# A Fourier-filter prologue and the last units of a two-matrix block: GpSimd and ScalarE steps moved earlier, sums reordered, filler products added

## The chip, the core and the metric

The kernel runs on one core of a Trainium2 chip. The core has five engines with a queue of instructions each: TensorE (PE in the profile; its weight loads are PEld) multiplies matrices into PSUM; VectorE (DVE) and ScalarE (ACT) work on PSUM and SBUF; GpSimd (POOL) works on SBUF; SyncE (SP) issues transfers. ScalarE and GpSimd issue transfers too. The metric is the device time of one execution in microseconds, as the median of several runs.

## What is computed

```python
def _attn_ref(x, filt_r, filt_i):            # x: (8, 3008, 256); filters: (1505, 256)
    X = np.fft.rfft(x, axis=1)
    F = (filt_r + 1j * filt_i)[None, :, :]
    return np.fft.irfft(X * F, n=x.shape[1], axis=1).astype(np.float32)

def _moe_ref(x, w_in, w_out):                # x: (24064, 256); w_in: (256, 2048); w_out: (2048, 256)
    h = x @ w_in
    g = h - np.tanh(h)
    return (g @ w_out).astype(np.float32)
```

The second function takes the first one's output, its eight batches laid end to end. The weights w_in and w_out arrive as 64-bit floats.

## The kernel before

**The transform.** A sequence of 3008 is 47 rows of 64. For each batch the transform runs in steps of small products: along the 64 ("first"), along the 47 ("forth"), the pointwise filter ("filtered"), and the two ways back ("back", "last"). The 32 frequencies along the 64 are cut into seven groups of five (`SLOTS`; the last has two, and its two halves of the columns are stacked, which gives 96 rows instead of 120). Group 0 to group 6 are handled one after the other.

**The prologue** does batch 0 with all data in SBUF, and ends where the main part begins. Per group g it issues, in this order: the loads of the filter rows of group g+2 (`filters_of`); the transposes of group g+2 (`across`, L1050, copied by L1054); the products of group g+1 (`there0`, L411 into the banks pa and pb; pa is copied by ScalarE, L414); the sum and difference of group g on VectorE (`next(there[g][0])`, L416 and L417, which read pb and the copy); three conversion steps (`convert(3)`); the filter of group g (`filtered`: L428, L433, L434, L435 on VectorE, then L437, by GpSimd for groups 1 to 4 and by VectorE for groups 0, 5 and 6; group 6 goes on with the sums L439 and L440); and the way back of the group before (`way_back`: L1087 and L1089 into the bank pe, copied by L1092, stored by L1093 to an array in memory). `back` (L459, L462, L464) does the same for group 6. Group 5's and group 6's ways back come last; then `rest` loads what all groups stored (L1077), four `first1` products of batch 1 run (L1175), 14 products that nobody reads (`warmer`, L1038) and the main part's first products (L576).

**The conversion** of the weights from 64 to 32 bits (`converted`) is a chain of steps per job of 512 words a row: a load (L174), one ScalarE step (L180), then VectorE steps L182, L185, L188, L191, L193 and a sum L200. `early` steps through the first five jobs, one step per call: five calls ahead of the group loop, behind group 0's transposes and in front of group 0's `there0`, three in each of groups 0 to 4, three at the start of group 5, and what is left behind the loop. `late` does the other jobs in the main part; there the ScalarE step of job k+1 is taken in the middle of job k.

**The filter rows turned.** Two rows of the last group come in the other order from memory, the imaginary one negated (`turned_rows`): GpSimd issues a load `neg` and one write (L531) ahead of the loop. At the end of group 2 VectorE negates (L540), GpSimd stores the result to `less` in memory (L541) and at once issues the write that reads `less` (L531). Two weight loads (`ahead`, L174) follow on GpSimd's queue. `filters_of(6)` reads what was written (L1067).

**The main part** is 192 units. Unit U multiplies by w_in (`up`, L617, seven products in place of eight), applies h - tanh h by an approximation (`shrink`: L729, L732, L735 on ScalarE, L739 on VectorE for each half of the columns, then four sums L597 to L600), and multiplies by w_out (`down`, L787, seven products). The stages of one unit overlap those of the next two: U's `up` is interleaved with U-1's `shrink` and U-2's `down` through the calls `d`, `e`, `s`, `t`. `steps_at` says how many steps of `shrink` run at each of eight places of `up`. The order of every engine's queue is that of the program. `down` collects four units in PSUM; the fourth ends with sums (L801 to L821), and the very last is turned and stored by `store_last` (L885, L886, L888).

What the change touches, in the names of the lines above: `weights` (L249), `turned_rows` (L540 to L542), `steps_at` (L626), `shrink` (ahead of L761), `down` (L798 to L821), `store_last` (L882 to L890), and the group loop (L1215 to L1236).

Of the kernel before, what the change touches and what calls it, by code (L numbers as in the profile page):

```python
# [18 lines left out]
NQ, NR = 64, 47  # L19
# [97 lines left out]
def kernel(  # L117
# [123 lines left out]
    def weights(tiles, jobs, queue, began, ahead, after=()):  # L241

        began += [begun(tiles, job, queue) for job in jobs[len(began):ahead]]
        yield
        for k in range(len(jobs)):
            pending[0] = len(jobs) - k
            for n, _ in enumerate(began[k]):
                yield
                if after and n == 2 and k + 1 < len(jobs):  # L249
                    next(began[k + 1])  # L250
            if k + ahead < len(jobs):
                began.append(begun(tiles, jobs[k + ahead], queue))
            pending[0] = len(jobs) - k - 1
            for u in dict(after).get(k, ()):
                yield from sums(u)
# [272 lines left out]
    def turned_rows(t):  # L528

        def turned_to(v, src, top):  # L530
            G.dma_start(dram(filt_d, (turned * 8 + 5 + 2 * v) * DM,  # L531
                             [[DM // 2, 2], [8 * DM, NH], [1, DM // 2]]),
                        dram(src, top * DM, [[DM // 2, 2], [(top > NH and -NQ or -1) * DM, NH],
                                             [1, DM // 2]]))

        G.dma_start(t, dram(filt_i.tensor, (SEQ // 2 - NQ * (NH - 1)) * DM,
                            [[NQ * DM, NH], [1, DM]]))
        turned_to(0, filt_r.tensor, SEQ // 2)
        yield
        V.tensor_scalar(out=t, in0=t, scalar1=-1.0, scalar2=None, op0=ALU.mult)  # L540
        G.dma_start(dram(less_d, 0, [[DM, NH], [1, DM]]), t)  # L541
        turned_to(1, less_d, NH - 1)  # L542
        yield

# [59 lines left out]
    def up(U, d, e, s, t):  # L604

        i, u = divmod(U, 4)
        b, tu, w = uts[i]
        rhs = [b[0][0], b[1][0], b[1][1], tu[:, 3, 0:w], tu[:, 0, 0:w], tu[:, 1, 0:w],
               tu[:, 2, 0:w]]
        banks = {k: ps.tile([128, 2, 256], F32, tag=k, bufs=1, name=k) for k in "xyz"}  # L610
        X, Y, Z = (banks[k][:, :, 0:w] for k in "xyz")
        h = dn.tile([128, 4, 2, 256], F32, tag="h", bufs=3, name="h")
        hs[U] = (h, w)

        def mm(bank, q, first):
            for k in range(2):
                nc.tensor.matmul(bank[:, k], wu[:, q - 1, (2 * u + k) * 128:(2 * u + k + 1) * 128],  # L617
                                 rhs[q - 1], start=(first and k == 0), stop=True,
                                 skip_group_check=True)

        def copied(tag):
            t = dn.tile([128, 2, 256], F32, tag=tag, bufs=1, name=tag)[:, :, 0:w]
            ACT.copy(t, X)  # L623
            return t

        steps_at = ([1, 1, 1, 1, 0, 1, 1, 0] if U > 1 else [0, 0, 1, 0, 2, 0, 2, 1])  # L626

        close = groups[i][0] == 0

        def shrinks(at):  # L630
            for _ in range(steps_at[at]):
                s()

        mm(X, 1, True)
        mm(Y, 2, True)
        s1 = copied("s1")
        t(0)
        d()
        shrinks(0)
# [12 lines left out]
        shrinks(3)  # L652
        e()
        t(2)
        mm(X, 7, False)
        u3 = copied("u3")
        V.tensor_add(h[:, 3, :, 0:w], Z, u3)  # L657
        shrinks(4)
        d()
        shrinks(5)  # L660
        e()
        if close:
            t(3)
        mm(X, 4, False)
        V.tensor_copy(h[:, 2, :, 0:w], X)  # L665
        if not close:
            t(3)
        shrinks(6)
        d()
        e()  # L670
        t(4)
        mm(Z, 3, False)
        V.tensor_add(h[:, 1, :, 0:w], Z, u2)  # L673
        shrinks(7)
# [42 lines left out]
    def shrink(U):  # L717
# [39 lines left out]
            return  # L757
        t = dn.tile([128, 4, 2, 256], F32, tag="t", bufs=2, name="t")
        blocks = [[h[:, 2 * a + k, :, 0:w] for k in range(2)] for a in range(2)]

        combine(blocks, [t[:, k, :, 0:w] for k in range(4)],  # L761
                V if pending or U + 2 >= 4 * len(groups) else G)
# [5 lines left out]
    def down(U):  # L768
# [24 lines left out]
        if done:  # L793
# [1 line left out]
                          for k in ("p1", "p5", "pu2"))  # L795
            o = dn.tile([128, 2, CH * 128], F32, tag="o", bufs=1, name="o")
            x12 = o[:, 0, w:2 * w]
        mm(1, 2)  # L798
        yield
        if done:  # L800
            ACT.copy(p1, product(1))  # L801
            V.tensor_add(o[:, 0, 0:w], product(2), p1)
        yield
        mm(3, 5)
        yield
        if done:
            ACT.copy(p5, product(5))
            V.tensor_add(x12, product(3), p5)
# [3 lines left out]
        if done:  # L812
            V.tensor_add(u2, product(6), p1)
            V.tensor_add(p1, product(7), u2)
            G.tensor_add(x12, u2, x12)  # L815
        yield
        mm(4)
        yield
        if done:
            V.tensor_add(o[:, 1, 0:w], product(4), p1)  # L820
            G.tensor_add(o[:, 1, w:2 * w], p1, p5)  # L821
            accs.pop(i)
            if i + 1 < len(groups):
                stores.append((i, o))
# [53 lines left out]
    def store_last(i, o):  # L878

        b, c = groups[i]  # L880
        ot = dn.tile([128, CH, DM], F32, tag="ot", bufs=1, name="ot")
        for h, copy in ((0, ACT.copy), (1, V.tensor_copy)):  # L882
            pt = psl([128, CH, 128], "xy"[h])
            for j in range(CH):
                nc.tensor.transpose(pt[:, j], o[:, h, j * 128:(j + 1) * 128], one)  # L885
            copy(ot[:, :, h * 128:(h + 1) * 128], pt)  # L886
        for (r, step, m, j, half), queue in zip(runs(c), (nc.sync, ACT)):
            queue.dma_start(dram(out.tensor, (b * SEQ + r) * DM,  # L888
                                 [[NR * DM, 64], [step * DM, m], [1, DM]]),
                            ot[64 * half:64 * half + 64, j:j + m])  # L890

    def store_some(n):
        for dst, src in outs[:n]:
# [95 lines left out]
    with tc.tile_pool(name="tr", bufs=2) as tr, tc.manual_schedule():  # L989
# [16 lines left out]
        with tc.tile_pool(name="pro", bufs=1) as pro, \  # L1006
# [201 lines left out]
            for g in range(last_g + 1):  # L1208
# [5 lines left out]
                    ones_1 = first1(load_x(big([128, 8, DM], F32, "x1"), 1, 0, 8))  # L1214
                if g == last_g - 1:  # L1215
                    under(fts[last_g])
                    convert(3)
                    way_back()
                if g < last_g:
                    there[g + 1] = there0(g + 1)  # L1220
                next(there[g][0])
                if g < last_g - 1:
                    convert(3)
                xy = there.pop(g)[1]
# [4 lines left out]
                if g in summed:  # L1229
                    next(chain)  # L1230
                ended.append((back, (0, g, xy, z0, (ACT, nc.sync))) if g in summed else (back0, (g, nn)))
                if g not in (0, last_g - 1):
                    way_back()
                if g == 2:
                    next(turning)
                    ahead = [begun(tiles1, job, queue=G) for job in jobs[5:7]]  # L1236
            rest(0, SG * (last_g - 1), [nc.sync])
            way_back()
            rest(SG * (last_g - 1), NA - SG * (last_g - 1), [nc.sync])
# [207 lines left out]
```

## Time and profile before

| | |
|---|---|
| median of 3 runs | 2564.09 us (2563.33 to 2565.52) |
| the profiled execution | 2566.24 us |
| its span, first to last instruction | 2564.4 us |
| mean granted TensorE clock | 0.996 |
| GpSimd busy | 58% |
| DMA, mean over the span | 83 GB/s |
| prologue (start to the first L576) | 87.6 us |
| the last store's issue | 2557.1 us |

A row of the timeline has start and duration in us, engine, line, operation, what is written and read, the shape, and in brackets the idle time of the engine ahead of it with what ended it. A row of waits has the total, the number and the longest. SPq, ACTq and POOLq are the queues that issue transfers. A 32-bit product of 256 columns shows as two records.

### The profile page before, as it was taken

The page shows a single profiled execution, that of the slowest core. Times are in us where ns is not written, and L with a number is a line of the kernel's source. Part 1 is how long each engine was busy: PE and PEld are TensorE (multiplying, and loading weights), DVE is VectorE, ACT ScalarE, POOL GpSimd, SP SyncE. Part 2 cuts the span into 40 slices and gives each one's busy share as a digit, 9 for nine tenths or more (in the row PEclk, how much of TensorE's full clock was granted, in tenths as well). Part 3 has the DMA queues.
Part 4 walks back from the last instruction along what each step waited for, and adds up shares of the span by engine and source line. Part 5 has one row for each costly group of instructions (what it writes and reads, how often), then busy time and mean ns, then how long its engine had stood idle before and what let it go on. Part 6 is the DMA issues. An engine that isn't in the chain of part 4 may idle for free.

```text
span 2564.4 us, 44624 instructions
## 1 busy us (share of the span) xinstructions
PE 2540.9 (99%) x17076; PEld 2177.8 (85%) x17076; DVE 1878.4 (73%) x2265; ACT 1666.3 (65%) x2497; POOL 1481.4 (58%) x1124
## 2 busy tenths in 40 slices
PE   8999999999999999999999999999999999999998
PEld 7678888888898888988888888898889888898887
DVE  6788776887678876788668886688866877555555
ACT  4566666666666666666666666676666666666665
POOL 4256665666466655666656665566645666555552
PEclk9999999999999999999999999999999999999999
DMA  8873214422343323342233322443123322110110
GB/s 221 260 198 103 65 35 109 119 67 48 76 118 93 80 54 94 82 108 67 72 94 90 92 67 61 101 105 97 36 64 88 93 66 52 26 32 18 26 21 19
DMA packets 333660, 212.43 MB, mean 83 GB/s; under 512 B 231737, under 2 KB 304855, under 8 KB 329789
## 3 DMA queue, kind: packets, MB, share of 16 engines
q1 hardware_dynamic: 318511, 184.59, 29.5%
q0 software_dynamic: 11424, 17.03, 2.4%
q10 hardware_dynamic: 3502, 7.87, 0.9%
q8 instruction: 136, 2.23, 0.4%
q14 instruction: 87, 0.71, 0.1%
HBM read 128.75 MB, written 83.39 MB: 83 GB/s over the span
## 4 chain that ended last, share of the span: by engine, by line
PE 94%; DMA 2%; DVE 1%; ACT 1%; issue 1%; POOL 0%; ACTq 0%; POOLq 0%; DVEq 0%
PE o L787 43%; PE x L617 25%; PE z L617 12%; PE y L617 6%; PE pm L401 3%; PE pu L576 2%; DMA ct<-a 1%; PE pm L340 1%; DMA raw<-in_moe_w_in_dram 0%; DMA fh<-f 0%; DMA mats_sb<-mats 0%; PE pe L1089 0%; PE o L842 0%; PE pf L297 0%; PE warm L1038 0%
## 5 line engine op out<-in xcount | busy, mean ns | idle before, releaser
L787 PE MATMUL o<-t,wd 128*128 128x256 f32 (+1 forms) x3008 | 763.6, 377 | 0.0
L597 POOL TENSOR_TENSOR t<-h 128x512 f32<-128x512 f32 (+1 forms) x186 | 305.7, 1643 | 712.4 <-DVE h L739 703.9
L739 DVE TENSOR_TENSOR h<-h,y 128x1024 f32<-128x1024 f32 (+1 forms) x384 | 579.8, 1510 | 160.8 <-ACT y L735 157.3
L787 PEld LDWEIGHTS o<-t,wd 128*128 128x128 f32 x3008 | 569.3, 190 | 85.3 <-POOL o L815 15.1
L617 PE MATMUL x<-tu,wu 128*128 128x256 f32 (+1 forms) x2256 | 576.2, 378 | 0.2 <-ACT u L623 0.2
L787 PE MATMUL o<-h,wd 128*128 128x256 f32 (+1 forms) x2256 | 573.6, 377 | 1.8 <-DVE h L739 1.8
L787 PEld LDWEIGHTS o<-h,wd 128*128 128x128 f32 x2256 | 426.0, 190 | 72.8 <-issue 18.4
L623 ACT COPY s<-x 128x512 f32<-128x512 f32 (+1 forms) x188 | 108.6, 578 | 564.6 <-PE x L617 564.6
L617 PEld LDWEIGHTS x<-tu,wu 128*128 128x128 f32 x2256 | 423.6, 190 | 57.2 <-issue 3.7
L732 ACT ACTIVATE y<-y 128x1024 f32<-128x1024 f32 (+1 forms) x384 | 399.4, 1040 | 12.1
L735 ACT ACTIVATE y<-y 128x1024 f32<-128x1024 f32 (+1 forms) x384 | 399.8, 1041 | 4.6
L729 ACT ACTIVATE y<-h 128x1024 f32<-128x1024 f32 (+1 forms) x384 | 400.5, 1043 | 3.6 <-DVE h L665 1.7
L598 POOL TENSOR_TENSOR t<-h,t 128x512 f32<-128x512 f32 (+1 forms) x186 | 313.9, 1688 | 14.6
L600 POOL TENSOR_TENSOR t<-h,t 128x512 f32<-128x512 f32 (+1 forms) x186 | 303.7, 1633 | 0.0
L599 POOL TENSOR_TENSOR t<-h 128x512 f32<-128x512 f32 (+1 forms) x186 | 289.7, 1557 | 0.0
L623 ACT COPY u<-x 128x512 f32<-128x512 f32 (+1 forms) x376 | 213.3, 567 | 57.0 <-PE x L617 53.7
L665 DVE COPY h<-x 128x512 f32<-128x512 f32 (+1 forms) x188 | 127.8, 680 | 127.2 <-PE x L617 127.1
L617 PE MATMUL z<-tu,wu 128*128 128x256 f32 (+1 forms) x752 | 190.2, 376 | 0.4 <-DVE h L673 0.4
L617 PE MATMUL z<-ut,wu 128*128 128x256 f32 (+1 forms) x752 | 190.2, 376 | 0.4 <-DVE h L657 0.4
L617 PE MATMUL y<-ut,wu 128*128 128x256 f32 (+1 forms) x752 | 190.2, 376 | 0.0
L617 PE MATMUL x<-ut,wu 128*128 128x256 f32 (+1 forms) x752 | 190.2, 376 | 0.0
L657 DVE TENSOR_TENSOR h<-z,u 128x512 f32<-128x512 f32 (+1 forms) x188 | 127.2, 677 | 72.1 <-ACT u L623 71.1
(198 smaller groups left out, 2815.7 us busy)
## 6 DMA issues: line engine op xcount, KB each, us to landing
ft<-filt SPq DMA_DIRECT2D x28, 1024.0 KB
ct<-nn SPq DMA_DIRECT2D x56, 512.0 KB
e<-ct SPq DMA_DIRECT2D x47, 512.0 KB
a<-ct SPq DMA_DIRECT2D x112, 192.0 KB
out_dram<-ot SPq DMA_DIRECT2D x1248, 16.0 KB
x_sb<-in_x_dram SPq DMA_DIRECT2D x110, 128.0 KB
ct<-a SPq DMA_DIRECT2D x60, 128.0 KB
ct<-x_sb SPq DMA_DIRECT2D x60, 128.0 KB
```

What stands on the lines that cost most here:

```text
L597: by.tensor_sub(t[0], b[0][1], b[0][0])
L598: by.tensor_sub(t[1], b[1][1], t[0])
L599: by.tensor_sub(t[2], b[1][1], b[0][1])
L600: by.tensor_sub(t[3], b[1][0], t[1])
L617: nc.tensor.matmul(bank[:, k], wu[:, q - 1, (2 * u + k) * 128:(2 * u + k + 1) * 128], rhs[q - 1], start=(first and k == 0), stop=True, ski ...
L623: ACT.copy(t, X)
L665: V.tensor_copy(h[:, 2, :, 0:w], X)
L729: ACT.activation(y[k], ht[k], AF.Arctan, scale=TURN)
L732: ACT.activation(y[k], y[k], AF.Tanh, scale=BEND)
L735: ACT.activation(y[k], y[k], AF.Square, scale=SCALE, accum_out=y_sums[:, 2 * U + k // 2:2 * U + k // 2 + 1])
L739: V.tensor_mul(ht[k], ht[k], y[k])
L787: nc.tensor.matmul(product(q), wd[:, q - 1, (2 * u + k) * 128: (2 * u + k + 1) * 128], rhs[q - 1][:, k], start=(u == 0 and k == 0 and q == ...
```

## The change

- `weights`: the ScalarE step of the next job is taken in the middle of the current one for the early jobs too, not only for the late ones.
- `turned_rows`: the negation runs on GpSimd, and the store of `less` and the write that reads it are in two steps. The first is called at the end of group 1, the second at the end of group 2. The two `ahead` loads are issued at group 3, in front of its `way_back`.
- Group 5: its L416 and L417 are issued first, then four filler products, then the way back of group 4; its three conversion steps move to its end, behind three more filler products.
- `steps_at` has a seventh step; it has work only in the last unit's `up`, where the four sums of the unit before come behind `up`'s last sum (L673).
- `down` of the last unit takes its products in the order 2, 3, 1, 5, 6, 7, 4; its sums follow, one of them moves from GpSimd to VectorE, and one GpSimd sum is issued earlier.
- `store_last` works by halves of the rows instead of halves of the columns: each is turned, copied and stored by two transfers, the second half of the rows first.

```diff
@@ weights
-                if after and n == 2 and k + 1 < len(jobs):
+                if n == 2 and k + 1 < len(jobs):
                     next(began[k + 1])
@@ turned_rows
         yield
-        V.tensor_scalar(out=t, in0=t, scalar1=-1.0, scalar2=None, op0=ALU.mult)
+        G.tensor_scalar(out=t, in0=t, scalar1=-1.0, scalar2=None, op0=ALU.mult)
         G.dma_start(dram(less_d, 0, [[DM, NH], [1, DM]]), t)
+        yield
         turned_to(1, less_d, NH - 1)
@@ up
-        steps_at = ([1, 1, 1, 1, 0, 1, 1, 0] if U > 1 else [0, 0, 1, 0, 2, 0, 2, 1])
+        steps_at = ([1, 1, 1, 1, 0, 1, 1, 1] if U > 1 else [0, 0, 1, 0, 2, 0, 2, 1])
@@ shrink
+        if U + 2 == 4 * len(groups):
+            yield
         combine(blocks, ...)
@@ down
-        mm(1, 2)
+        last_unit = U + 1 == 4 * len(groups)
+        mm(*((2, 3) if last_unit else (1, 2)))
         yield
-        if done:
+        if done and not last_unit:
             ACT.copy(p1, product(1))
             V.tensor_add(o[:, 0, 0:w], product(2), p1)
         yield
-        mm(3, 5)
+        mm(*((1, 5) if last_unit else (3, 5)))
         yield
+        if last_unit:
+            ACT.copy(p1, product(1))
+            V.tensor_add(o[:, 0, 0:w], product(2), p1)
...
-            G.tensor_add(x12, u2, x12)
+            (V if last_unit else G).tensor_add(x12, u2, x12)
+            if last_unit:
+                G.tensor_add(o[:, 1, w:2 * w], p1, p5)
...
-            G.tensor_add(o[:, 1, w:2 * w], p1, p5)
+            if not last_unit:
+                G.tensor_add(o[:, 1, w:2 * w], p1, p5)
@@ store_last
-        for h, copy in ((0, ACT.copy), (1, V.tensor_copy)):
-            pt = psl([128, CH, 128], "xy"[h])
-            for j in range(CH):
-                nc.tensor.transpose(pt[:, j], o[:, h, j * 128:(j + 1) * 128], one)
-            copy(ot[:, :, h * 128:(h + 1) * 128], pt)
-        for (r, step, m, j, half), queue in zip(runs(c), (nc.sync, ACT)):
...
+        for lo, tag, copy in ((2, "x", ACT.copy), (0, "y", V.tensor_copy)):
+            pt = psl([128, 2, DM], tag)
+            for h in range(2):
+                for j in range(2):
+                    nc.tensor.transpose(pt[:, j, h * 128:(h + 1) * 128],
+                                        o[:, h, (lo + j) * 128:(lo + j + 1) * 128], one)
+            copy(ot[:, lo:lo + 2], pt)
+            for (r, step, m, j, half), queue in zip(runs(c), (nc.sync, ACT)):
...
@@ the group loop
                 if g == last_g - 1:
                     under(fts[last_g])
-                    convert(3)
+                    next(there[g][0])
+                    warmer(4)
                     way_back()
                 if g < last_g:
                     there[g + 1] = there0(g + 1)
-                next(there[g][0])
+                if g != last_g - 1:
+                    next(there[g][0])
...
+                if g == 3:
+                    ahead = [begun(tiles1, job, queue=G) for job in jobs[5:7]]
                 if g not in (0, last_g - 1):
                     way_back()
-                if g == 2:
+                if g in (1, 2):
                     next(turning)
-                    ahead = [begun(tiles1, job, queue=G) for job in jobs[5:7]]
+                if g == last_g - 1:
+                    warmer(3)
+                    convert(3)
```

More of the change, by code (lines that the diff above doesn't have):

```diff
@@ L881, in store_last @@
         ot = dn.tile([128, CH, DM], F32, tag="ot", bufs=1, name="ot")
-        for h, copy in ((0, ACT.copy), (1, V.tensor_copy)):
-            pt = psl([128, CH, 128], "xy"[h])
-            for j in range(CH):
-                nc.tensor.transpose(pt[:, j], o[:, h, j * 128:(j + 1) * 128], one)
-            copy(ot[:, :, h * 128:(h + 1) * 128], pt)
-        for (r, step, m, j, half), queue in zip(runs(c), (nc.sync, ACT)):
-            queue.dma_start(dram(out.tensor, (b * SEQ + r) * DM,
-                                 [[NR * DM, 64], [step * DM, m], [1, DM]]),
-                            ot[64 * half:64 * half + 64, j:j + m])
+        for lo, tag, copy in ((2, "x", ACT.copy), (0, "y", V.tensor_copy)):
[6 more added lines that the diff above has]
+            for (r, step, m, j, half), queue in zip(runs(c), (nc.sync, ACT)):
+                queue.dma_start(dram(out.tensor, (b * SEQ + r + step * lo) * DM,
+                                     [[NR * DM, 64], [step * DM, 2], [1, DM]]),
+                                ot[64 * half:64 * half + 64, j + lo:j + lo + 2])
     def store_some(n):
```

## The prediction

> **What bounds the kernel now.** I read the page first, then the waits of TensorE, then the granted clock by microsecond, then the timeline of the prologue (0 to 88 us) and of the last 25 us.
>
> ```profile
> PE 2540.9 (99%) x17076; PEld 2177.8 (85%) x17076; DVE 1878.4 (73%) x2265; ACT 1666.3 (65%) x2497; POOL 1481.4 (58%) x1124
> ...
> PE 94%; DMA 2%; DVE 1%; ACT 1%; issue 1%; POOL 0%; ACTq 0%; POOLq 0%; DVEq 0%
> ...
> PE pe L1089 <- POOL nn L437: 5.4, 2, 4.3
> PE pe L1087 <- DVE nn L434: 1.8, 1, 1.8
> ```
>
> TensorE is busy for 99% of the span and 94% of the chain. A change that takes no product away can win only TensorE's idle time and its slow time. The idle time that lies late in the prologue is in the rows above (one pause of 4.3 us, one of 1.8 us); one more pause of 1.56 us, shown below, lies at the very end. The slow time is in the windows (columns: busy time and count of PE, PEld, DVE, ACT, POOL, then granted clock, DMA share, GB/s):
>
> ```profile
> 56.00:57.00 1.00, 0.00 (x0) 0.00 (x0) 1.00 (x1) 0.00 (x0) 1.00 (x1) 0.74 0.88 191
> ...
> 63.00:64.00 1.00, 1.00 (x6) 0.81 (x5) 0.00 (x0) 0.42 (x1) 0.32 (x1) 0.84 0.17 42
> ...
> 70.00:71.00 1.00, 0.43 (x3) 0.17 (x2) 0.96 (x3) 0.00 (x0) 0.09 (x1) 0.57 0.90 135
> ...
> 76.00:77.00 1.00, 1.00 (x4) 0.66 (x3) 0.96 (x2) 0.00 (x0) 0.00 (x0) 0.52 0.61 213
> ```
>
> After each prologue pause the clock halves (at about 56.5 and 70.1) and comes back at about 63.3 and 77.0, so two stretches of about 6.8 us run at 0.50. Where the first pause comes from:
>
> ```profile
> 53.73 0.68 POOL L531 DMA_DIRECT2D filt<-less  x1 [5.17 <-DMA less<-neg]
> 53.83 0.68 DVE L188 SCALAR_TENSOR_TENSOR top<-raw,top 128x512 int32<-128x512 int32 x1
> ...
> 55.00 2.72 DVE L193 SCALAR_TENSOR_TENSOR low<-raw,low 128x512 f32<-128x512 uint32 x1
> ...
> 55.88 1.29 POOL L437 TENSOR_TENSOR nn<-nn,xy 120x512 f32<-120x512 f32 x1
> ...
> 57.22 0.47 PEld L1089 LDWEIGHTS pe<-nn,mats_sb 120*120 120x120 f32 x2 [4.67 <-POOL nn L437]
> ...
> 57.65 1.21 DVE L428 TENSOR_TENSOR nn<-xy,filt 120x1024 f32<-120x1024 f32 x1
> ...
> 60.23 0.68 DVE L435 TENSOR_TENSOR xy<-xy,filt 120x512 f32<-120x512 f32 x1
> ...
> 64.75 0.66 DVE L182 TENSOR_SCALAR top<-top 128x512 f32<-128x512 f32 x1 [3.24 <-ACT top L180]
> ...
> 65.34 0.67 DVE L416 TENSOR_TENSOR xy<-pb,xy 120x512 f32<-120x512 f32 x1
> ```
>
> GpSimd stood 5.17 us behind its own store of the negated filter rows. Group 3's sum (L437) and two loads were queued behind that, TensorE behind the sum. Meanwhile VectorE's L193 took 2.72 us beside the sum, and then VectorE idled 3.24 us for a ScalarE conversion step (L180). So VectorE, which runs almost without gaps from 28 to 62 us, sets the pace of the groups.
>
> **Filter rows one group ahead.** The negation (on GpSimd), the store of its result and the write that reads it back are now in three groups' turns instead of one, with a group between store and read. Groups follow each other every 7.2 us (four of them from L428 at 28.86, quoted below, to L428 at 57.65), more than the 5.17 us wait, so nothing of it is left, or at most a fraction of a microsecond. The store and the negation join GpSimd's queue in group 1 behind L437 and two stores of results; nobody waits for these soon. The two weight loads move from group 2 to group 3; they are first used by the main part's conversions. Worth: TensorE's 4.3 us, the half clock after it, and L193's stretch (2.72 for 0.69, so 2.0 us). Bounds for that last: nothing, if the stretch comes again beside another GpSimd sum, up to 2.0. I take 2.0, because after the move L437 stands beside L416 and L417, which read PSUM.
>
> **ScalarE steps ahead.** This is where a cost appears. L180 of the next job is now issued before the fourth VectorE step of the current one. The second job's L180 therefore moves from group 0's turn into the five steps ahead of the loop, in front of group 0's L414 on ScalarE's queue.
>
> ```profile
> 23.39 0.66 ACT L180 ACTIVATE top<-raw 128x512 f32<-128x512 f32 x1
> ...
> 25.26 0.59 ACT L414 COPY xy<-pa 120x512 f32<-120x512 f32 x1 [1.20 <-PE pa L411]
> ...
> 26.19 0.69 DVE L416 TENSOR_TENSOR xy<-pb,xy 120x512 f32<-120x512 f32 x1
> ...
> 28.86 1.22 DVE L428 TENSOR_TENSOR nn<-xy,filt 120x1024 f32<-120x1024 f32 x1
> ...
> 31.09 0.68 ACT L180 ACTIVATE top<-raw 128x512 f32<-128x512 f32 x1 [1.66 <-DMA raw<-in_moe_w_in_dram]
> ```
>
> ScalarE waited for that job's raw weights to land until 31.09, even at the later place. At the new place ScalarE stands from 24.05 to 31.09, then converts until 31.77, and group 0's L414 ends at 32.36 instead of 25.85. Queued behind it are the copies of groups 1 and 2; VectorE's L416 waits for L414, and TensorE, which needs the copies, runs dry for some 5 us in its turn.
>
> [...]
>
> VectorE then runs L416, L417 and three conversion steps before L428. Spacings between starts, from these rows: L185 0.45, L188 0.73, L191 0.46; a pair of operations of 0.69 takes 1.33, as L188 (0.73) and, further below, L437 to L416 (0.61, 70.08 to 70.69) show: so L416 with L417, and L193 with L200; L182 0.45 as L185.
>
> ```profile
> 74.69 0.42 DVE L185 TENSOR_SCALAR top<-top 128x512 int32<-128x512 int32 x1
> ...
> 75.14 0.69 DVE L188 SCALAR_TENSOR_TENSOR top<-raws,top 128x512 int32<-128x512 int32 x1
> ...
> 75.87 0.43 DVE L191 TENSOR_SCALAR low<-top 128x512 int32<-128x512 int32 x1
> ...
> 76.33 0.69 DVE L193 SCALAR_TENSOR_TENSOR low<-raws,low 128x512 f32<-128x512 uint32 x1
> ```
>
> Group 0's L428 starts at 32.40 + 1.33 + 1.33 + 0.45 = 35.51 instead of 28.86: **6.65 late**. Bounds: 0 (data there by 24.05) and 7.7 (31.77 less 24.05). I take the full 6.65, since nothing ahead of the load changes.
>
> What is won back on VectorE:
>
> ```profile
> 45.15 0.28 DVE L540 TENSOR_SCALAR neg<-neg 24x256 f32<-24x256 f32 x1
> ...
> 47.80 0.47 DVE L182 TENSOR_SCALAR top<-top 128x512 f32<-128x512 f32 x1 [1.05 <-ACT top L180]
> ...
> 70.08 0.69 DVE L437 TENSOR_TENSOR nn<-nn,xy 120x512 f32<-120x512 f32 x1
> 70.69 0.41 DVE L416 TENSOR_TENSOR xy<-pb,xy 96x256 f32<-96x256 f32 x1
> ...
> 74.36 0.41 DVE L440 TENSOR_TENSOR xy<-nn 96x256 f32<-96x256 f32 x1
> ...
> 76.95 1.05 PE L459 MATMUL pe<-xy,mats_sb 96*96 96x128 f32 x8
> ```
>
> Groups 1 to 3: L540 leaves (0.2); group 3's wait of 1.05 and two steps (0.93) become three steps (1.64), 0.3 less. Late by 6.1. Group 4: from L188 at 53.83 to L428 at 57.65 was 3.82; now three steps, 1.78. Late by 4.1. **Sixth group's sums first:** L416 of group 5 stood 5.11 us after L435 (65.34 less 60.23) behind an add, a ScalarE wait and a step; now it follows at 0.61 (as 70.08 to 70.69), so 4.5 less: 0.4 early. The three steps come back ahead of the last group's L416: 1.64, so 1.2 late, and L440 ends at 76.0 instead of 74.8.
>
> But TensorE's last product of the prologue's groups (L459) did not wait for L440 before: it started at 76.95 because the product ahead of it ran at half clock. With the clock up, and **the filler products** (7, each two records of about 0.22 us going by the ten in 2.43 us at 2548.12 below, all in time that would be idle) to keep it there, it waits for L440 only. L459 starts at 76.0: **0.95 us won**. From there to the main part TensorE runs without a pause (products, then filler), so the shift is passed on.
>
> **Last units.**
>
> ```profile
> 2542.76 0.68 DVE L673 TENSOR_TENSOR h<-z,u 128x512 f32<-128x512 f32 x1
> ...
> 2543.36 1.22 DVE L739 TENSOR_TENSOR h<-h,y 128x1024 f32<-128x1024 f32 x1
> ...
> 2543.48 1.06 ACT L729 ACTIVATE y<-h 128x1024 f32<-128x1024 f32 x1 [1.06 <-DVE h L673]
> ...
> 2548.12 2.43 PE L787 MATMUL o<-h,wd 128*128 128x256 f32 x10 [1.56 <-DVE h L739]
> ...
> 2556.34 0.69 DVE L886 COPY ot<-pt 128x512 f32<-128x512 f32 x1 [1.13 <-PE pt L885]
> 2557.09 0.50 SPq L888 DMA_DIRECT2D out_dram<-ot  x1
> ...
> 2560.00:2561.00 1.00, 0.00 (x0) 0.00 (x0) 0.00 (x0) 0.00 (x0) 0.00 (x0) 0.50 0.61 192
> ```
>
> L673 goes ahead of the four sums, so the last L739 starts 1.06 earlier. The last unit begins with products 2 and 3, which need only the half that L739 finished at 2544.58. TensorE's 1.56 us wait goes; the eight records of those two take 1.7 us, which covers the other half (three ScalarE steps of 1.06 from 2542.42 and 1.23 of L739: 2546.9, an estimate). At the end the output leaves in two halves. The second is issued where the whole was, after a copy of 0.69; the first, copied meanwhile by ScalarE, about one copy sooner. The bytes are the same, and their transfer is still under way 3 us after the issue (last row), so it ends about 0.6 sooner. Taken: 1.56 + 0.6 = **2.2**; bounds 1.5 (four DMAs of shorter rows eat the lead) to 2.6 (L739's earlier start also shortens the end).
>
> **Sum.** 0.95 + 2.2 = 3.2 us. The profiled execution took 2566.24 us (span 2564.4 and 1.8 around it): 2563.1. It lies 2.15 above the median of the runs, 2564.09; from that, **2560.9 us**.
>
> **Rivals.**
> 1. *ScalarE's early wait costs nothing* (the data land in time, or the delay is absorbed). For it: only L180's row shows the landing. Against: there ScalarE had nothing else to wait for. The prologue gives 0.95 + 6.65 = 7.6: 2564.1 - 7.6 - 2.2 = **2554.3**.
> [...]
> 3. *Slower: the early stall is not won back.* The later gaps on VectorE close only if nothing else takes their place; if GpSimd's stores or the store's landing, 6 us later as well, hold group 4's and 5's sums as now, the 6.65 stay and the three steps ahead of the last group add 1.64: 2564.1 + 6.65 + 1.64 - 2.2 = **2570.2**. It decides once L459 starts later than 76.95 + 5.1 + 2.2 = 84.3. Against: of the two gaps, one hung on the read-back alone and one on the step that moved.
> 4. *The prologue's shift is swallowed later.* The DMA engines are full (next row), and chains through the first batches' stores run there. Only the tail counts: **2561.9**.
>
> ```profile
> 110.00:120.00 10.00, 10.00 (x32) 5.72 (x31) 9.38 (x16) 7.20 (x13) 7.60 (x12) 1.00 1.00 355
> ```
>
> **Chances.** Forecast 0.48 (its own range 2557.5 to 2564), rival 1 0.25, rival 2 0.10, rival 3 0.12, rival 4 0.05. About 0.2%, 5.1 us, is what a measurement of this kernel can tell from no change. Faster than 2559.0: rival 1 and 0.08 of the forecast, 0.33. Slower than 2569.2: rival 3 and 0.02, 0.14. Between: 0.53. The range takes in rivals 1, 2 and 4 and most of what lies between them and rival 3: 2552.5 to 2567.5.
>
> **What would show it.** Right: a second L180 on ScalarE at about 31 with some 7 us idle ahead of it, group 0's L416 near 32.4, no GpSimd wait over 1 us at L531, L416 of group 5 within 1 us of L435, L459 near 76, the last unit's first product without a wait. Wrong: that L180 before 26 (rival 1), the clock at 0.50 after 66 (rival 2), L459 after 84 (rival 3).

## The result and the profile after

| | before | after |
|---|---|---|
| median of 19 runs each, in turns | 2565.28 us (2563.33 to 2568.14) | 2568.92 us (2565.4 to 2573.66) |
| ratio after to before, 95% interval | | 1.0014 (1.0008 to 1.0021) |
| the profiled execution | 2566.24 us | 2573.66 us |
| its span | 2564.4 us | 2571.8 us |

The change makes the kernel 3.6 us slower; 2560.9 us and a gain were forecast, and 2568.92 lies above the range. The profiled execution of after is the highest of its 19 runs, 4.7 us above their median: what is read from it shows where time goes, and sizes are taken from the runs further down.

The page of after, busy time and the shares of the chain that ended last:

```profile
PE 2542.4 (99%) x17090; PEld 2176.1 (85%) x17090; DVE 1877.0 (73%) x2265; ACT 1666.5 (65%) x2497; POOL 1481.2 (58%) x1124
...
PE 94%; DMA 3%; DVE 2%; issue 0%; ACT 0%; SPq 0%; POOL 0%; ACTq 0%; DVEq 0%; POOLq 0%
```

TensorE is busy 1.5 us longer, the filler and the slower clock included, and DMA's and VectorE's shares of the chain grew by one point each. The timeline of after, the three engines' rows one engine after the other, shows the prologue:

```profile
30.71 0.66 ACT L180 ACTIVATE top<-raw 128x512 f32<-128x512 f32 x1 [7.22 <-DMA raw<-in_moe_w_in_dram]
31.27 0.58 ACT L414 COPY xy<-pa 120x512 f32<-120x512 f32 x1
...
31.88 0.69 DVE L416 TENSOR_TENSOR xy<-pb,xy 120x512 f32<-120x512 f32 x1 [6.28 <-ACT xy L414]
...
34.88 1.22 DVE L428 TENSOR_TENSOR nn<-xy,filt 120x1024 f32<-120x1024 f32 x1
...
63.75 0.68 DVE L435 TENSOR_TENSOR xy<-xy,filt 120x512 f32<-120x512 f32 x1
64.36 0.68 DVE L416 TENSOR_TENSOR xy<-pb,xy 120x512 f32<-120x512 f32 x1
...
65.80 1.22 DVE L428 TENSOR_TENSOR nn<-xy,filt 120x1024 f32<-120x1024 f32 x1
...
77.99 0.69 DVE L428 TENSOR_TENSOR nn<-xy,filt 96x512 f32<-96x512 f32 x1 [4.73 <-DMA filt<-filt]
...
80.41 0.42 DVE L439 TENSOR_TENSOR xy<-nn 96x256 f32<-96x256 f32 x1
...
54.23 0.67 POOL L531 DMA_DIRECT2D filt<-less  x1
...
80.97 1.99 PE L459 MATMUL pe<-xy,mats_sb 96*96 96x128 f32 x8 [3.94 <-DVE xy L439]
```

Four of the six forecast signs are there: the second L180 at 30.71 behind 7.22 us of waiting, group 0's L416 at 31.88 and its L428 at 34.88 (35.51 was worked out), no GpSimd wait at L531, and group 5's L416 at 0.61 after L435. A fifth, in the last unit, follows below. The sixth is not there: L459 starts at 80.97 and not near 76. In front of it stands a wait that no step of the prediction names: VectorE stands 4.73 us for the filter rows of group 6. The queue of SP shows how they come to be late, first before, then after:

```profile
57.94 0.34 SPq L1067 DMA_DIRECT2D filt<-filt  x1
58.32 1.63 SPq L1070 DMA_DIRECT2D filt<-in_filt_r_dram  x4
59.99 2.38 SPq L1070 DMA_DIRECT2D filt<-in_filt_i_dram  x4
62.66 0.72 SPq L1060 DMA_DIRECT2D a<-a  x1
64.20 0.64 SPq L1060 DMA_DIRECT2D filt<-filt  x1
```

```profile
60.36 0.33 SPq L1079 DMA_DIRECT2D filt<-filt  x1
60.74 1.54 SPq L1082 DMA_DIRECT2D filt<-in_filt_r_dram  x4
62.33 5.44 SPq L1082 DMA_DIRECT2D filt<-in_filt_i_dram  x4
68.12 0.72 SPq L1072 DMA_DIRECT2D a<-a  x1
71.08 0.64 SPq L1072 DMA_DIRECT2D filt<-filt  x1
```

The read-back of the turned rows is issued 2.4 us later (60.36 for 57.94), the eight loads behind it take 7.0 us of issue instead of 4.1, and the copy that makes the last group's rows complete goes out 6.9 us later (71.08 for 64.20) and lands at 77.99. The windows say what is in the way (columns as in the prediction's):

```profile
60.00:70.00 10.00, 7.93 (x36) 6.00 (x34) 9.73 (x15) 2.15 (x4) 5.08 (x7) 1.00 1.00 278
...
77.00:78.00 1.00, 0.03 (x1) 0.00 (x0) 0.01 (x1) 0.59 (x1) 0.00 (x0) 1.00 0.95 333
78.00:79.00 1.00, 0.00 (x0) 0.00 (x0) 0.97 (x2) 0.00 (x0) 0.00 (x0) 1.00 0.82 252
...
81.00:82.00 1.00, 1.00 (x5) 1.00 (x6) 0.96 (x3) 0.00 (x0) 0.00 (x0) 0.50 0.27 101
...
86.00:87.00 1.00, 1.00 (x3) 0.76 (x3) 0.00 (x0) 0.58 (x1) 0.00 (x0) 0.50 0.75 258
87.00:88.00 1.00, 1.00 (x6) 0.87 (x5) 0.00 (x0) 0.30 (x2) 0.00 (x0) 0.95 0.66 141
```

From 60 to 70 us the DMA engines are busy all the time (share 1.00): the rows share them with batch 1's data and the two moved weight loads. TensorE is without work from 77.0 to 81.0; its clock falls to 0.50 at 80.3 and is back at 1.00 at 87.1.

From L459 to the main part's first product it is 13.70 us after (80.97 to 94.67) and 10.65 before (76.95 to 87.60). So the prologue of this execution ends 7.1 us later: 4.0 at L459 and 3.05 by the clock (half of the 6.1 us from 80.97 to 87.1). A later landmark is the main part's third group of the products L577 (L576 before), first before, then after:

```profile
245.43 1.16 PE L576 MATMUL pu<-gt,e 64*64 64x64 f32 x64
```

```profile
253.98 1.16 PE L577 MATMUL pu<-gt,e 64*64 64x64 f32 x64
```

There after is 8.55 us behind; 1.5 us more went between 95 and 254 us. The end of the kernel gives some back (after):

```profile
2554.97 2.32 PE L790 MATMUL o<-h,wd 128*128 128x256 f32 x10
...
2563.09 0.58 ACT L898 COPY ot<-pt 128x512 f32<-128x512 f32 x1 [4.10 <-PE pt L896]
2563.53 0.69 DVE L898 COPY ot<-pt 128x512 f32<-128x512 f32 x1 [1.46 <-PE pt L896]
2563.70 2.26 SPq L900 DMA_DIRECT2D out_dram<-ot  x2
2563.71 2.27 ACTq L900 DMA_DIRECT2D out_dram<-ot  x2
```

The last unit's first product has no wait (1.56 before), which is the fifth sign. From the landmark to the end it is 2317.8 us (2571.8 less 253.98), against 2319.0 before (2564.4 less 245.43). The sum closes: 8.55 less 1.2 is the 7.4 us between the two spans.

### The profile page after: what moved, and what is told of

The parts are those of the page before. It is cut to its first block, busy times and chain, and to the rows that moved or that the text cites. A ratio compares the mean times of both kernels' runs of the same rounds, so it can differ in the third digit from the quotient of the medians.

```text
span 2571.8 us, 44655 instructions
## 1 busy us (share of the span) xinstructions
PE 2542.4 (99%) x17090; PEld 2176.1 (85%) x17090; DVE 1877.0 (73%) x2265; ACT 1666.5 (65%) x2497; POOL 1481.2 (58%) x1124
## 4 chain that ended last, share of the span: by engine, by line
PE 94%; DMA 3%; DVE 2%; issue 0%; ACT 0%; SPq 0%; POOL 0%; ACTq 0%; DVEq 0%; POOLq 0%
PE o L790 44%; PE x L618 25%; PE z L618 12%; PE y L618 6%; PE pm L401 3%; PE pu L577 2%; DMA ct<-a 1%; PE pm L340 1%; PE o L852 0%; DMA raw<-in_moe_w_in_dram 0%; DMA fh<-f 0%; PE pf L297 0%; DMA mats_sb<-mats 0%; DMA filt<-filt 0%; DMA x<-in_x_dram 0%
## 5 line engine op out<-in xcount | busy, mean ns | idle before, releaser
L618 PE MATMUL x<-tu,wu 128*128 128x256 f32 (+1 forms) x2256 | 575.9, 378 | 0.0
L618 PEld LDWEIGHTS x<-tu,wu 128*128 128x128 f32 x2256 | 423.0, 190 | 57.3 <-issue 3.7
L618 PE MATMUL y<-ut,wu 128*128 128x256 f32 (+1 forms) x752 | 190.1, 375 | 1.1 <-ACT a L299 1.1
L618 PE MATMUL z<-tu,wu 128*128 128x256 f32 (+1 forms) x752 | 190.1, 375 | 0.4 <-DVE h L674 0.4
L618 PE MATMUL z<-ut,wu 128*128 128x256 f32 (+1 forms) x752 | 190.1, 375 | 0.4 <-DVE h L658 0.4
L618 PE MATMUL x<-ut,wu 128*128 128x256 f32 (+1 forms) x752 | 190.1, 375 | 0.0
```

## Experiments

Two theories stood at the start. A: the ScalarE step in front of group 0's L414 is the cost. B: the removed waits were worth little, since the last group's filter rows take their place. Beside them it was open whether the last units lose where the prediction had a gain. The expectations of e5 to e7 set two more against each other, C and D. Every run below was timed in turns with the kernel before on the same chip; before's medians are 2564.68 (first four runs), 2565.51 (next four), 2565.12 (e9 to e12), 2565.29 (e13, e14) and 2565.53 (e15, e16). The difference in brackets is to that median.

**e1 and e2: the step taken back.** The whole change, with the early jobs' ScalarE step late as before (e1), or only the first one late (e2).

```diff
-                if n == 2 and k + 1 < len(jobs):
+                if after and n == 2 and k + 1 < len(jobs):          # e1
+                if (after or k) and n == 2 and k + 1 < len(jobs):   # e2
```

> The changed kernel with the early jobs' ScalarE steps back in their old places. Theory A (the loss begins at the second job's L180, which stands 7.2 us ahead of group 0's L414, and all that is late behind it follows from that): group 0's L428 starts near 28.9 instead of 34.9, the copied filter rows of group 6 are there before L428 of group 6 wants them (wait under 1 us instead of 4.7), L459 near 72 instead of 81, the main part's first L577 near 83, the time 2556 to 2561. Theory B (the loss is the chain of group 6's filter rows itself: negation on GpSimd, write, read-back, loads, copy, whatever stands ahead): group 6's L428 still waits 3 us or more and the time stays within 2566 to 2570.

> The changed kernel in which only the second job's ScalarE step is back in its old place; those of the third to fifth job stay ahead. Theory A: as the run with all steps in the old places or up to 1 us faster, since those steps find their data landed: L428 of group 0 near 28.9, L459 70 to 73, the time 2555 to 2561. Theory B: group 6's L428 still waits 3 us or more, 2566 to 2570.

Measured: e1 2564.13 (-0.6), ratio 0.9998 (0.9989 to 1.0007); e2 2563.47 (-1.2), 0.9997 (0.9988 to 1.0006). So one instruction, the first early L180, carries the loss: without it the change is level with before. But it is no gain of 7 us either: the time lies between those of the two theories, and neither had it. In e2's timeline the last group's L428 still waits 4.5 us for a transfer, at 72.04.

**e3: the step alone.** Before with the change's line in `weights` and nothing else.

```diff
-                if after and n == 2 and k + 1 < len(jobs):
+                if n == 2 and k + 1 < len(jobs):
```

> The kernel before with the early ScalarE steps moved ahead and nothing else. Theory A: ScalarE stands about 7 us ahead of the second L180 near 31, group 0's L428 starts near 35 instead of 28.9, of the 6 us only some 3 come back at VectorE's ScalarE waits (1.05 and 3.24), the GpSimd wait at L531 stays, the time 2567 to 2573. Theory B: the early delay is absorbed by the pauses that lie later anyway, within 2 us of the kernel before.

Measured: 2571.21 (+6.5), 1.0025 (1.0015 to 1.0035). So the step alone makes the kernel before slower by more than the whole change does. The timeline, VectorE's row and then GpSimd's, shows the waits that the rest of the change takes away:

```profile
60.62 3.35 DVE L428 TENSOR_TENSOR nn<-xy,filt 120x1024 f32<-120x1024 f32 x1
...
59.40 0.68 POOL L531 DMA_DIRECT2D filt<-less  x1 [5.17 <-DMA less<-neg]
```

GpSimd waits the same 5.17 us as before, here 5.7 us later, and VectorE's L428 takes 3.35 us instead of 1.22 beside GpSimd's work.

**e4, e8, e10 and e11: the last units alone.** The kernel before with the change's `steps_at`, `shrink`, `down` and `store_last` (e4, and e11 again), and with `store_last` left as before (e8, and e10 again).

> The kernel before with the last units' new order alone. From the two traces the last sums start 8.6 us late and the last instruction ends 7.4 us late, so the end has won 1.2: 1.0 to 2.3 us faster than before. If the output in four smaller transfers eats what TensorE gains, within 0.5 us of the kernel before.

> The kernel before with the last units' new order, but the output turned and stored in the old two transfers. If the halves in four transfers give back what they lead by (from the trace of the changed kernel, where the second pair is issued more than 1 us after its copy): as fast as the whole new order or faster, 1.5 to 2.3 us under the kernel before. If the halves win as the prediction had it (0.6): 0.5 to 1 us slower than the whole new order, 1.0 to 1.6 us under the kernel before.

> The kernel before with the last units' new order but the output stored whole, beside the next run on the same chip. If the two halves cost what the late second pair of DMA issues suggests (about 1 us), this one is 0.5 to 1.5 us faster than the next: about 2562.6. If the halves are worth the 0.6 us that the prediction gave them, it is 0.6 slower than the next.

> The same with the output stored in two halves: about 2563.4 if the halves cost about 1 us, about 2562.0 if they win 0.6.

Measured: e4 2562.94 (-1.7), 0.9995 (0.9986 to 1.0004); e8 2562.74 (-2.8), 0.9987 (0.9978 to 0.9996); e10 2563.29 (-1.8) and e11 2563.45 (-1.7), both 0.9995 (0.9986 to 1.0004). So the new order of the last units wins about 2 us, and the loss does not lie there. e8's 2.8 is more than either of its expectations gave; e10, the same kernel again, has 1.8. Two halves or a whole: e10 and e11, on one chip, differ by 0.2, within the scatter.

**e5, e6 and e7: room for the filter rows.** e2 with the two loads `ahead` issued at the end of group 5 instead of group 3 (e5), with batch 1's rows issued in group 5 behind `under` (e6), with both (e7).

```diff
-                if g == 3:
-                    ahead = [begun(tiles1, job, queue=G) for job in jobs[5:7]]
                 if g == last_g - 1:
                     warmer(3)
                     convert(3)
+                    ahead = [begun(tiles1, job, queue=G) for job in jobs[5:7]]   # e5, e7
@@ e6, e7
-                    ones_1 = first1(load_x(big([128, 8, DM], F32, "x1"), 1, 0, 8))
                 if g == last_g - 1:
                     under(fts[last_g])
+                    ones_1 = first1(load_x(big([128, 8, DM], F32, "x1"), 1, 0, 8))
```

> The changed kernel with the second job's ScalarE step in its old place, and with the two weight loads of GpSimd's queue issued at the end of group 5 instead of in group 3. Theory C (group 6's filter rows are late because they share full DMA engines with the megabyte of batch 1's rows and the megabyte of those two loads): the eight loads of group 6's rows take 4 to 5 us instead of 7.2, their copy is issued near 61 instead of 65.4, VectorE's L428 of group 6 waits under 1.5 us instead of 4.5, L459 starts 70 to 72 instead of 75, the time 2557 to 2561. Theory D (the chain write, read-back, loads, copy has its own latencies, whatever else moves): no change against the run without this move, 2562 to 2565.

> As the run with only the second ScalarE step put back, but batch 1's rows (1 MB on SyncE's queue) are issued in group 5 behind the copy of group 6's rows instead of in group 3. Theory C: the eight loads of group 6's rows take 4 to 5 us, L428 of group 6 waits under 1.5 us, L459 70 to 72, unless the rows themselves land too late for the first products of batch 1 near 74; the time 2557 to 2562. Theory D: 2562 to 2565.

> Both moves together. Theory C: the loads of group 6's rows in 3 to 4.5 us, no wait of L428 in group 6, L459 69 to 71; the two megabytes now land between 64 and 75, where the stores and loads of the ways back run, so the main part's first L577 gains less, 79 to 83; the time 2556 to 2561. Theory D: 2562 to 2565.

Measured: e5 2563.89 (-1.6), 0.9992 (0.9983 to 1.0001); e6 2564.56 (-1.0), 0.9994 (0.9985 to 1.0004); e7 2566.07 (+0.6), 1.0002 (0.9993 to 1.0011). e5's TensorE rows:

```profile
69.75 1.09 PE L459 MATMUL pe<-xy,mats_sb 96*96 96x128 f32 x8
...
83.36 0.33 PE L577 MATMUL pu<-gt,e 64*64 64x64 f32 x4 [3.03 <-DMA e<-ct]
```

Theory C holds for the wait and not for the time. With room, the eight loads take 5.6, 3.1 and 3.2 us of issue in e5, e6 and e7 (7.1 in e2), and L459 comes at 69.0 to 69.8 in all three: 7 us before the 76.95 of before's profiled run, and 2 to 4 us before e4, e8 and e10, which have before's prologue (72.0 to 73.2). Then TensorE stands 2.6 to 5.2 us for the tables of the main part's first products (L577, `rest`), and the time hardly moves.

**e9: the prologue alone**, with the last units as before. **e12:** e5 with the output stored whole.

> The changed kernel's whole prologue (early ScalarE step, rows one group ahead, sixth group's sums first, filler) with the last units as before. Theory: the early step costs about 5 to 6 us, the removed pauses win back next to nothing net, since the sixth group's filter rows take their place: 2565.3 + 5.5 = 2570.8, ratio 1.0015 to 1.0030. Rival (the prologue is worth what the first median said, 2568.92 plus the predicted 2.2 of the last units): 2571.1 - the same; a rival that the cost lies in the last units instead: no more than 2566.

> All of the change but the first early ScalarE step and the halves, with the two loads ahead moved behind group 5: the best parts together. If parts add up: 2563.9 less 1.0, about 2562.8 where before is at 2565.5, and no faster than the last units' order alone, because the main part's first products wait for batch 2's conversion tables whatever the prologue gains. If the prologue's gain (the last group's sum 5 to 7 us sooner) is passed on: 2558 to 2560.

Measured: e9 2571.4 (+6.3), 1.0019 (1.001 to 1.0028); e12 2566.16 (+1.0), 1.0001 (0.9992 to 1.001). e9 agrees with the runs of the last units: they hide some 2.7 us of the prologue's loss (6.3 less 3.6). e12 missed: it was to be at 2562.8, and parts that look like gains do not add up.

**e13 and e14: the step kept, room for the rows.** After with e5's edit (e13) and with e6's (e14).

> The changed kernel, the first early ScalarE step included, with the two loads ahead issued behind group 5 instead of group 3. Theory (the early step's delay reaches TensorE mainly through the last group's filter rows, which come behind full DMA engines): the copy of those rows lands by about 71, L428 of the last group and L459 follow VectorE at about 73 and 76 (the 76.0 of the prediction), L577 at 86 to 87, time 2564 to 2566. Rival (the delay of 6 us runs straight down VectorE's and SP's order, with the loads only a bystander): L459 at 79 or later, L577 at 92 or later, time 2568 to 2570.

> The changed kernel with batch 1's rows (1 MB) issued in group 5 behind its own copy instead of in group 3. Theory: the last group's store and eight loads no longer share the engines with them, the copy of its rows is issued by 67 instead of 71.1, L459 at 76 to 77, L577 at 86 to 88, time 2564 to 2567. Rival (straight delay): L459 at 79 or later, time 2568 to 2570.

Measured: e13 2569.56 (+4.3), 1.0016 (1.0007 to 1.0025); e14 2569.68 (+4.4), 1.0018 (1.0009 to 1.0027). e13's timeline:

```profile
33.72 1.21 DVE L428 TENSOR_TENSOR nn<-xy,filt 120x1024 f32<-120x1024 f32 x1
...
73.98 1.09 PE L459 MATMUL pe<-xy,mats_sb 96*96 96x128 f32 x8
...
75.56 3.16 SPq L464 DMA_DIRECT2D ct<-e  x2
...
84.00 1.46 SPq L1089 DMA_DIRECT2D e<-ct  x4
...
87.95 0.33 PE L577 MATMUL pu<-gt,e 64*64 64x64 f32 x4 [3.38 <-DMA e<-ct]
```

The place came out as the first theory had it, or earlier (L459 at 73.98 here and 73.15 in e14, for 76), and the time as its rival did. L428 of the last group has no wait. Then the last group's results are stored (75.56), the second of SP's two stores goes out at 78.38, the tables' last load follows at 84.00, and TensorE waits for it until 87.95; without the step, in e5, the same load went out at 79.85. So against e5 the step's delay is passed on whole: 4.5 us at group 0's L428 (29.25 in e5), 4.2 at L459, 4.6 at L577.

**e15 and e16: the two loads behind the tables**, on SP. e15 is without the first early step and stores the output whole; e16 is after.

```diff
             rest(SG * (last_g - 1), NA - SG * (last_g - 1), [nc.sync])
+            ahead = [begun(tiles1, job, queue=nc.sync) for job in jobs[5:7]]
```

> The change without the first early ScalarE step and with the output stored whole, and the two loads ahead (1 MB) issued on SP behind the last load of batch 2's tables, not on GpSimd's queue. If full engines hold the last tables (in two runs 4 to 6 us from the last group's store to its landing), that store lands 2 to 3 us sooner: L577 waits at most 1 us for tables and starts at 80 to 82, time 2561 to 2563. If the chain of store, wait and load on SP takes that long without other traffic, L577 stays at 83 to 85 and the time at 2564 to 2566.

> The changed kernel, its first early ScalarE step included, with the same move of the two loads. If the step's delay reaches the main part through full engines ahead of the last tables, the tables are there by 85 and the time falls to 2564 to 2566. If the delay is passed straight on (the last group's product, its store, its load, each as late as the first group was), L577 stays at 86 to 88 and the time at 2568 to 2570.

Measured: e15 2566.26 (+0.7), 1.0 (0.9991 to 1.0009); e16 2570.01 (+4.5), 1.0015 (1.0006 to 1.0024). Again the place moved as expected and the time did not. Rows of e15's timeline:

```profile
80.57 0.33 PE L577 MATMUL pu<-gt,e 64*64 64x64 f32 x4 [0.63 <-DMA e<-ct]
...
106.12 1.07 ACT L299 COPY a<-pf 128x512 f32<-128x512 f32 x2 [3.50 <-DMA ct<-a]
106.76 3.38 PE L297 MATMUL pf<-x_sb,f 128*128 128x256 f32 x8 [4.87 <-ACT a L299]
...
246.82 1.16 PE L577 MATMUL pu<-gt,e 64*64 64x64 f32 x64
```

and its windows:

```profile
36.00:100.00 64.00, 60.03 (x323) 45.22 (x322) 50.10 (x85) 24.53 (x44) 18.18 (x22) 1.00 0.80 220
...
96.00:120.00 24.00, 19.13 (x58) 11.58 (x57) 15.81 (x27) 17.08 (x29) 10.95 (x17) 0.93 1.05 298
```

This prologue is all that the change could ask for: full clock from 36 to 100 us, and the main part starts at 80.57, 7 us before the profiled run of before and 2 to 3 us before e8, e10 and e4 (82.76 to 83.86). At 106 us TensorE stands 4.87 us for a ScalarE copy that itself waits for a store, with the DMA engines full (1.05), and the third group starts at 246.82: 1.4 us later than before's 245.43. In e16 the main part's first products wait for nothing, at 84.71; TensorE then waits 2.6 us at L297 for a transfer and 3.0 in two waits at L618 behind ScalarE.

**All profiled runs at the landmark.** The start of the third group of products splits an execution: what lies ahead is prologue and the stage with full DMA engines, what lies behind is the rest and the last units. One profiled execution each:

| | ahead of it, mean | ahead of it, each |
|---|---|---|
| prologue of before (before, e4, e8, e10, e11) | 244.6 | 245.4, 243.6, 242.5, 243.9, 247.8 |
| changed, without the first early step (e1, e2, e5, e6, e7, e12, e15) | 246.3 | 245.6, 249.2, 244.5, 244.7, 246.5, 246.7, 246.8 |
| with it (after, e3, e9, e13, e14, e16; e3 without the rest of the change) | 249.5 | 254.0, 248.3, 249.4, 249.0, 246.7, 249.4 |

| | behind it, mean | lowest and highest |
|---|---|---|
| last units of before (before, e3, e9) | 2319.3 | 2319.0 to 2319.5 |
| new order, stored in halves (11 runs) | 2317.3 | 2316.9 to 2317.8 |
| new order, stored whole (e8, e10, e12, e15) | 2317.6 | 2316.9 to 2318.1 |

The last units win 2.0 us, and the halves are not told from the whole. The early step costs about 3 us here, and 4.8 by the medians (after's +3.6 less e2's -1.2, each against its own before). Pairs that differ by the step alone show its delay arriving: at group 0's L428, at the main part's first product and at the landmark it is 6.0, 5.8 and 4.8 us in after against e2, 4.5, 4.6 and 4.6 in e13 against e5, and 4.3, 3.5 and 2.0 in e14 against e6. The rest of the changed prologue is no gain either: without the step it reaches the landmark some 1.6 us later than the prologue of before (246.3 for 244.6), within the scatter, and the medians say the same (0.3 us under before on average in these seven runs, 2.0 with the new last units alone). Which of its edits costs this was not separated. The same prologue of before varies by 5.3 us from one execution to the next.

## Why the prediction was wrong, point by point

**What bounds the kernel.** The rows were read rightly for one execution, and the kernel does not always run so. Its two half-clock stretches and its L459 at 76.95 were taken as the kernel's. Of the five profiled executions with this prologue one more has them (e11, L459 at 76.87); in e4, e8 and e10 the mean clock from 56 to 96 us is 0.96 and not 0.83. e8 has L459 here:

```profile
72.04 1.11 PE L459 MATMUL pe<-xy,mats_sb 96*96 96x128 f32 x8 [0.38 <-DVE xy L439]
```

and its first L576 at 82.76, 4.8 us before that of the profiled run. A gain measured against the stretches was partly a gain that other executions of this prologue already have. The three runs' median, 2564.09, was also 1.2 us under that of the 19.

**Filter rows one group ahead.** Right in what it removes: the wait at L531 is gone in each run with it. L193's stretch went too: after, the L437 of group 3 (57.82, 1.26 us) stands beside L416 and L417, which take 0.62 and 0.69 us, and L193 takes 0.68. The worth of it all was mis-sized: e1, e2 and e5 to e7 have it and are no faster than the last units' new order alone (e4, e8, e10, e11).

**ScalarE steps ahead.** Right in mechanism: ScalarE's L414 stood behind the L180 that waited 7.22 us, as the order of its queue had it. In this execution the size was near too: 6.65 us at group 0's L428 were worked out, 6.0 came (34.88 less 28.86). But it is the largest of six: in the other executions with the step L428 starts between 31.15 (e9) and 34.55 (e3), 2.3 to 5.7 us late, depending on when the second job's weights are there. The full 6.65 was near the upper end. That VectorE is level with before again by group 5 was right. After starts group 5's L428 at 65.80 (above), and before here:

```profile
66.77 1.22 DVE L428 TENSOR_TENSOR nn<-xy,filt 120x1024 f32<-120x1024 f32 x1
```

But it is level only by the waits that the other edits take away: against e2, e5 and e6, which have these edits and not the step, little of the delay is made up by the main part's start (the pairs above).

**L459.** This is the step that failed: "it waits for L440 only. L459 starts at 76.0: 0.95 us won". The working on VectorE was good: without its 4.73 us wait for the rows, L459 would have started at 76.24. But the transfers of group 6's filter rows were a term put at nothing without a reason; the part on the turned rows stopped at the store and the read on GpSimd's queue, and did not follow SP's read-back, eight loads and copy, each 2 to 7 us later, into a stretch with full DMA engines. In place of "L440 only" the runs show that wait for the rows: 4.73 us after, and none in e5 and e13, where there is room. (L428 also waits 4.49 us in e2 and 3.73 in e9; there the profile names another transfer of SP's queue, `e<-ct`.)

**"From there to the main part TensorE runs without a pause."** This was wrong as well, and it is why mending L459 mends no time. Behind L459 stand a store, a load of tables (e5, e13) and a stage with full engines (e15, e16), and each takes over when the one ahead of it goes. In the prediction's own terms: the other prologue edits were to win 7.6 us (0.95 + 6.65, as rival 1 has it) and to pay for the step. The runs show nothing of that win at the landmark (246.3 for 244.6), while the step costs 4.8 by the medians and the last units win 2.0. So the gains that were set against the step's cost end ahead of the landmark, and the cost does not; why it does not stays open (below). Rival 4, that the shift is swallowed later, comes nearest to the runs without the step; it was given 0.05. Rival 3 came nearest to the measured time, with 2570.2, and by luck: its place was the store's landing at groups 4 and 5, these were on time, and L459 at 80.97 lies under its 84.3. Rival 1 fell at L180; rival 2's sign, the clock at 0.50 after 66, came from 80.3 to 87.1, but behind the wait for the rows: TensorE's pause for group 4's L437, 1.25 us up to 65.90, left the clock at 1.00.

**Why the step costs where a stall elsewhere does not.** One view bears on this, the window from 24 to 56 us. First e5, without the step, then e13, which differs from it by the step alone:

```profile
24.00:56.00 32.00, 30.02 (x158) 24.75 (x159) 30.89 (x48) 15.85 (x29) 15.59 (x20) 1.00 0.75 199
```

```profile
24.00:56.00 32.00, 27.17 (x139) 22.32 (x139) 27.39 (x42) 14.28 (x27) 12.71 (x18) 0.95 0.59 165
```

With the step, 34 GB/s less over 32 us, 1.09 MB, has been moved by 56 us, since transfers are issued in the order of work that is late. The stage from 96 to 160 us moves some 0.28 MB a microsecond (282 and 283 GB/s), so the arrears are worth 3.8 us, an estimate, near the 4.6 us between the landmarks of e5 and e13. By this sum a pause of TensorE without late transfers would leave no arrears.

Other runs do not follow this sum. e6, without the step, has moved 0.45 MB less than e5 in the same window (185 GB/s), and its landmark is no later (244.7 for 244.5). e14, with the step, has 169 GB/s and its landmark at 246.7; e9, with the step but only 2.3 us late at group 0's L428, has 188 GB/s and 249.4. The bytes moved by 96 us fit better: over all 18 profiled executions their correlation with the landmark is -0.84, and that of the main part's start is 0.79. But any delay lowers the one and raises the other. That late transfers are what the step costs is argued and not shown.

**Last units.** Right: 2.2 forecast, 2.0 measured. The 0.6 for the halves was too much: at most 0.3, within the scatter. (Ten records in 2.43 us are 0.24 us each and not 0.22; the eight cover L739's other half all the more.)

What stays open is which chain of stores and loads between 95 and 160 us sets the end of that stage. Of all versions, the kernel before with the new order of the last units and the whole store (e8) is the fastest measured, by 2.8 us and, again as e10, by 1.8; of the faster versions only e8's interval excludes no change.

## What to carry to other kernels

Before a wait is priced as a gain, follow the same group's transfers to their landing on every queue, and the next stage's as well: here three limits lay within a few microseconds of each other, and removing two won nothing. A step put ahead in an engine's queue is checked at the landing of its data first (ScalarE stood 7.22 us here, with L414 behind it); a stall that also delays the issue of transfers may come back where the DMA engines are full later, which these runs suggest and do not show. And one profiled execution may be off by as much as the whole forecast: a landmark deep in the kernel, compared over several executions, separates the parts better than the total.

## What had not been expected of the hardware

- The landing of one 512 KB load varied between executions with the same early step: ScalarE's second L180 started at 30.71 after, 28.72 in e14 and 26.87 in e9, after waits of 7.22, 4.23 and 2.89 us.
- Eight small loads (7 KB the smallest) took 7.0 us to issue on SP with a DMA share of 1.00, and 4.1 before with a share of 0.80 (58.3 to 62.4 us).
- VectorE's L428 took 3.35 us in e3 and L193 2.72 before, against 1.22 and 0.69, with GpSimd issuing loads and then adding in SBUF beside them.
